# w2·h as seven products in the transform's stream, and gate/up over both token groups in one pass

## The chip, the cores and the metric

One core of a Trainium2 chip. The metric is device time in microseconds of one execution. Every matmul has 128-row operands, 512 moving columns and float32 data, taken as a high and a low float32r part: a product of two float32 tiles is three matmuls (high·high, high·low, low·high).

## The reference

```python
g = sigmoid((x * gate_w).sum(-1, keepdims=True))     # x: 2048 tokens x 512
a = Cr @ (x @ Dr.T) - Ci @ (x @ Di.T)                # C: 2048 x 2048, D: 512 x 512
b = (silu(x @ w1) * (x @ w3)) @ w2                   # w1, w3: 512 x 1376; w2: 1376 x 512
out = g * a + (1 - g) * b
```

## The kernel before, in words

Products are done in Winograd's form of Strassen's scheme: seven products of half-size blocks instead of eight, with sums of blocks as operands and sums of results behind them.

*Gate/up.* x is cut into two groups of 1024 tokens, w1 and w3 into NC = 11 chunks of 128 columns (the last is padded; the padding holds gate_w, so the scores for g come out of it). An item is one chunk and one group: seven products, 42 matmuls in PSUM tiles X, Y, Z, and ends in a tile h of 128 x 1024. `load_w`, `prep_wa` and `prep_wb` fetch and split an item's weight forms; `first1` and `first2` run its first two products three items (`LOOK`) ahead, `second` the other five. `split` writes a high part on ScalarE and a low part on VectorE. One operand set `XO` of x is kept, that of the current group.

*Down.* After the items of a group, `down(g)` runs w2·h in plain form: 11 chunks, each 8 accumulators (tile acc) x 3 matmuls, 264 matmuls a group. h (kept in SBUF) is split in `prep_dn`; the split w2 is kept in DRAM (`w2sp`) for the second group. acc is multiplied by 1 - g and stored to `nbsp`. Beside the first `down` the x operands of group 1 are made (x1 to x3), beside the second the x forms of the transform (`load_a`), the gates, and the first loads of its stream.

*The stream.* The transform runs as six blocks, `STEPS` in order: four F blocks (x with 512 columns of C, results to `zsp` in DRAM) and two Y blocks (hidden transform of what lies in zsp, plus nbsp, to out). A block has seven products P1, P5, P6, P3, P7, P2, P4 (Y blocks: P1, P2, P5, ...), a product NQ steps (4 in F, 2 in Y), a step 12 matmuls (2 banks x 2 slices of the contraction x 3). After step m `advance` issues loads for step m + 8 (`load_c`), sums for m + 4 (`sum_c`), and the split for m + 3 (`split_c`, into tile zo, four in turn). Loads go to tiles of the pool f4 (`wide`), 13 in turn. Operand names are B11, B12, B21, B22 (blocks), and T1 to T4 (sums). T1 is made by a load of B12 and an accumulating transfer of B11 on top, issued from POOL (F blocks: by VectorE); T2 and T4 are then summed in T1's tile by VectorE. P6 takes T2, P7 T3, P4 T4. `forms1` and `forms2` make the stationary forms (4 for P1, P5, P6, P3, 3 for P2, P4, P7).

*Order.* When the kernel is built, each engine's instructions are put in a queue by when their inputs and tiles should be ready, not strictly in program order. On the chip each queue runs in order. A new tile waits for the last use of the one whose place it takes. Loads are issued from SP's queue, accumulating transfers from POOL's.

The lines that the steps hang on:

```python
ORDER = [CHAIN] * NTB + [tuple(CHAIN[i] for i in (0, 5, 1, 2, 3, 4, 6))] * (NTB // 2)
NEED = [(("B11", 0, 0), ("B12", 1, 1), ("B22", 2, 1), ("B21", 5, 0))] * NTB + [
    (("B11", 0, 0), ("B21", 1, 0), ("T1", 2, 6), ("B22", 3, 1), ("T3", 5, 6))] * (NTB // 2)
LEAD = 3
AHEAD = 5
```

NEED lists for each load the product at which it is wanted and how many steps earlier it is put in.

Of the kernel before, what the change touches and what calls it, by code (L numbers as in the profile page):

```python
# [23 lines left out]
NC2 = (NC + 1) // 2  # L24
WARM = 11


@with_exitstack
def fnet_swiglu_gate_kernel(
# [18 lines left out]

    nc = tc.nc
# [13 lines left out]
    f4 = ctx.enter_context(tc.tile_pool(name="f4", bufs=13, side="right"))  # L63
    dn_cm, dn = pool("dn", 2, "right")
    xo_cm, xo = pool("xo", 1, "left")
    wo_cm, wo = pool("wo", 2, "left")
    tp_cm, tp = pool("tp", 2, "left")
# [3 lines left out]

    def wide(name):
        return f4.tile([P, 1024], F32, tag="f4", name=name)
# [13 lines left out]
    gsp = dram.tile([2, P, 1024], F32, tag="gsp", name="gsp")  # L87
    dsp = [dram.tile([KD, P, 2, n, 256], F32, tag=f"dsp{n}", name=f"dsp{n}") for n in (4, 3)]
    w2sp = dram.tile([NC, P, 2, 512], F32, tag="w2sp", name="w2sp")
    zsp = dram.tile([4 * NTB * P, 1024], F32, tag="zsp", name="zsp")  # L90

# [3 lines left out]
    def forms1(r, m, t1):  # L95

        r, m = (v.rearrange("p (a n) -> p a n", a=4) for v in (r, m))
        a21, a11, a12, a22 = (r[:, i] for i in range(4))  # L100
        nc.vector.tensor_sub(m[:, 0], a22, a21)
        for d, v, w in ((1, m[:, 0], a11), (2, a12, m[:, 1])):
            nc.vector.scalar_tensor_tensor(m[:, d], v, -1.0, w, op0=ALU.mult, op1=ALU.subtract)
        split(t1[:, 0, 0], t1[:, 1, 0], a11)
        split(flat(t1[:, 0, 1:4]), flat(t1[:, 1, 1:4]), flat(m[:, 0:3]))
# [8 lines left out]
    def prep_d(p):  # L114

        r, m = wide(f"dr{p}"), wide(f"dm{p}")
        t1 = dn.tile([P, 2, 4, 256], F32R, tag="ho", name=f"d1_{p}")
        t2 = dn.tile([P, 2, 4, 256], F32R, tag="ho", name=f"d2_{p}")[:, :, :3]
        nc.sync.dma_start(r, dd[p])
        forms1(r, m, t1)  # L120
        forms2(r, t2)
        nc.sync.dma_start(dsp[0][p], t1.bitcast(F32))
        nc.sync.dma_start(dsp[1][p], t2.bitcast(F32))


# [6 lines left out]
    def load_xo(g, k):  # L132

        if g not in XO:
            XO[g] = xo.tile([P, 2, 7, 2, 512], F32R, tag="xo", name=f"xo{g}")
        ST[g, k] = wide(f"xs{g}_{k}")
        nc.sync.dma_start(ST[g, k], xt[g, XRAW.index(k)])
# [4 lines left out]
    def sum_xo(g, k):  # L142
        ST[g, k] = wide(f"xs{g}_{k}")
        nc.vector.tensor_sub(ST[g, k], *(ST[g, v] for v in SUMS[k]))
# [6 lines left out]
    LOOK = 3  # L151

    def load_w(i, lo=0, hi=4, queue=nc.sync):
        if lo == 0:
            WS[i] = wo.tile([P, 4, 256], F32, tag="ws", name=f"ws{i}", bufs=LOOK + 1)
        queue.dma_start(WS[i][:, lo:hi].rearrange("p a n -> p (a n)"),
                          w13[i % NC, :, lo * 256 : hi * 256])

    def prep_wa(i, lo=0, hi=3):

        if lo == 0:
            WA[i] = wo.tile([P, 2, 3, 256], F32R, tag="wa", name=f"wa{i}", bufs=LOOK + 1)
        t = WA[i]
        split(t[:, 0, lo:hi].rearrange("p a n -> p (a n)"),
              t[:, 1, lo:hi].rearrange("p a n -> p (a n)"),
              WS[i][:, lo:hi].rearrange("p a n -> p (a n)"))

    def prep_wb(i, part=None):

        if part != 1:  # L170
            w = WS.pop(i)
            u = wo.tile([P, 4, 256], F32, tag="wu", name=f"wu{i}", bufs=1)
            nc.vector.tensor_add(u[:, 0], w[:, 3], w[:, 2])
            nc.vector.tensor_sub(u[:, 1], u[:, 0], w[:, 0])
            nc.vector.tensor_sub(u[:, 2], w[:, 0], w[:, 3])
            nc.vector.tensor_sub(u[:, 3], w[:, 1], u[:, 1])
            WB[i] = u
        if part != 0:
            u = WB[i]
            t = wo.tile([P, 2, 4, 256], F32R, tag="wb", name=f"wb{i}")  # L180
            split(t[:, 0].rearrange("p a n -> p (a n)"), t[:, 1].rearrange("p a n -> p (a n)"),
                  u.rearrange("p a n -> p (a n)"))
            WB[i] = t

    def prod(ps, i, wi, xi, start, chain=False):
        g = i // NC
        w, wi = (WA[i], wi) if wi < 3 else (WB[i], wi - 3)
        x = XO[g]
# [5 lines left out]
    G, H = {}, {}  # L194

    def first1(i):
        x = bank(i % 4, f"X{i}")
        prod(x, i, 0, 0, True)
        s1 = tp.tile([P, 512], F32, tag="s1", name=f"s1_{i}", bufs=LOOK + 2)
        nc.scalar.activation(s1, x, AF.Copy)  # L200
        G[i] = (x, s1)

    def first2(i):

        y = bank(4 + i % 2, f"Y{i}")
        prod(y, i, 1, 1, True)
        s1 = G[i][1]
        nc.vector.tensor_add(s1, s1, y)  # L208
        put_score(i, 0, s1)
# [4 lines left out]
    def put_score(i, j, gate):  # L214


        if i % NC < NC - 1:
            return
        if j == 0:
            SC[i] = tp.tile([P, 2, 512], F32, tag="sc", name=f"sc{i}", bufs=1)  # L220
        nc.scalar.activation(SC[i][F % P :, j], gate[F % P :], AF.Copy)
        if j == 1:
            nc.sync.dma_start(gs[2 * (i // NC) : 2 * (i // NC) + 2].rearrange("b o n -> o b n"),
                              SC[i][F % P : F % P + 1])

    def second(i, between):
        x, s1 = G.pop(i)
        z = bank(6 + i % 2, f"Z{i}")
        u2 = tp.tile([P, 512], F32, tag="u2", name=f"u2_{i}")
        u4 = tp.tile([P, 512], F32, tag="u4", name=f"u4_{i}")  # L230
        g1 = tp.tile([P, 512], F32, tag="g1", name=f"g1_{i}")
        h = wide(f"h{i}")
        H[i] = h
        prod(x, i, 4, 4, False, True)
        nc.scalar.activation(u2, x, AF.Copy)  # L235
        prod(z, i, 5, 5, True, True)
        nc.scalar.activation(u4, z, AF.Copy)
        between[0]()
        prod(x, i, 3, 3, False, True)
        nc.vector.tensor_add(u4, u4, x)  # L240
        prod(z, i, 2, 6, False, True)
        nc.vector.tensor_add(u2, u2, z)  # L242
        nc.vector.tensor_mul(h[:, :512], s1, u2)
        between[1]()
        prod(x, i, 6, 2, False, True)
        put_score(i, 1, x)
        nc.scalar.activation(g1, x, AF.Silu)  # L247
        nc.vector.tensor_mul(h[:, 512:], g1, u4)

    HO, W2R, W2O = {}, {}, {}  # L250

    def load_w2(i):

        if NC <= i < 2 * NC:
            W2O[i] = f4.tile([P, 2, 512], F32R, tag="f4", name=f"w2o{i}")
            nc.gpsimd.dma_start(W2O[i].bitcast(F32), w2sp[i - NC])

    def prep_dn(i):
        g, c = divmod(i, NC)
        if g == 0 and c % 2 == 0:  # L260
            n = min(2, NC - c)
            r = wide(f"w2r{i}")
            nc.sync.dma_start(r[:, : n * 512], w2[c // 2, :, : n * 512])
            W2R[i // NC, c // 2] = r
        if g == 0:
            o = dn.tile([P, 2, 512], F32R, tag="w2o", name=f"w2o{i}")
            split(o[:, 0], o[:, 1], W2R[g, c // 2][:, (c % 2) * 512 : (c % 2 + 1) * 512])
            nc.sync.dma_start(w2sp[c], o.bitcast(F32))
            W2O[i] = o
        t = dn.tile([P, 2, 1024], F32R, tag="ho", name=f"ho{i}")  # L270
        split(t[:, 0], t[:, 1], H.pop(i))
        HO[i] = t

    def down(g, extra):
        e = g * NC + NC - 1
        late = [6 + (e + 1) % 2, 6 + e % 2, e % 4]
# [458 lines left out]
```

## Time and profile before

| | before |
|---|---|
| median of three runs | 726.28 us (726.05 to 726.74) |
| profiled execution | 726.83 us |
| its span, first to last instruction | 725.0 us |
| TensorE busy, matmuls | 718.4 us, 3149 |
| VectorE, ScalarE, POOL busy | 542.6, 357.4, 27.1 us |
| moved by DMA | 136.60 MB |

In lines of groups the columns are: source line, engine, operation, output<-inputs with shapes, count | busy us in total, mean ns of one | idle time ahead of them and what ended it. Matmuls overlap, so the 389 ns of one is its latency, not its pace.

### The profile page before, as it was taken

What the parts mean: (1) busy time and instruction counts of PE and PEld (TensorE: products, weight loads), DVE (VectorE), ACT (ScalarE), POOL (GpSimd) and SP (SyncE); (2) the same over time, 40 slices, a digit from 0 to 9 for tenths busy, and PEclk for the clock granted to TensorE, in tenths of its full rate; (3) what the DMA queues carried; (4) which work ended last, traced back from release to release, by engine and by line L of the source; (5) the groups of instructions that cost most, each with busy time, mean ns of one, the idle gap of its engine ahead of it and who ended that gap; (6) DMA issues with size and microseconds to landing.
All of it is one profiled execution on the core that took longest, in us unless ns stands there. A gap on an engine that the chain in (4) does not pass through costs nothing.

```text
span 725.0 us, 8409 instructions
## 1 busy us (share of the span) xinstructions
PE 718.4 (99%) x3149; PEld 589.5 (81%) x3149; DVE 542.6 (75%) x676; ACT 357.4 (49%) x460; POOL 27.1 (4%) x39
## 2 busy tenths in 40 slices
PE   8999999999999999999999999999999999999997
PEld 5888878888888878888888888888888888888886
DVE  6987786584499974588978986687759785667875
ACT  6655454454466642553656345444444444445451
POOL 0000000000000000100010001000100001000000
PEclk9999999999999999999999999999999999999999
DMA  6112135733056601786897734874296719999932
GB/s 260 59 59 87 54 108 215 288 133 146 30 192 231 244 30 42 249 320 257 331 269 244 254 139 79 240 244 148 39 240 214 215 21 231 369 372 308 336 152 87
DMA packets 38780, 136.60 MB, mean 188 GB/s; under 512 B 4050, under 2 KB 4178, under 8 KB 37716
## 3 DMA queue, kind: packets, MB, share of 16 engines
q1 hardware_dynamic: 33412, 117.20, 45.3%
q0 software_dynamic: 5040, 18.35, 11.5%
q8 instruction: 24, 0.39, 0.2%
q10 hardware_dynamic: 288, 0.52, 0.2%
q14 instruction: 16, 0.13, 0.1%
HBM read 105.12 MB, written 30.94 MB: 188 GB/s over the span
## 4 chain that ended last, share of the span: by engine, by line
PE 90%; DMA 3%; DVE 3%; ACT 2%; issue 1%; SPq 0%; ACTq 0%; DVEq 0%
PE P L81 53%; PE acc L81 14%; PE X L81 13%; PE Z L81 6%; PE Y L81 3%; PE C L81 1%; DMA dsp<-d 1%; DMA xr<-xn 1%; DMA xs_B<-xt 1%; DMA gt<-gs 1%; ACT wb L76 0%; DVE ho L77 0%; DVE s L208 0%; DVE d L77 0%; DVE u L242 0%
## 5 line engine op out<-in xcount | busy, mean ns | idle before, releaser
L81 PE MATMUL P<-zo,a 128*128 128x512 f32 x1344 | 304.8, 389 | 0.0
L81 PEld LDWEIGHTS P<-zo,a 128*128 128x128 f32 x1344 | 252.2, 188 | 52.5 <-DVE zo L77 0.2
L76 ACT ACTIVATE zo<-B 128x1024 fp32r<-128x1024 f32 x124 | 131.3, 1060 | 148.2 <-PE P L81 142.0
L77 DVE TENSOR_TENSOR zo<-B,zo 128x1024 fp32r<-128x1024 f32 x124 | 150.7, 1222 | 65.9 <-ACT zo L76 65.3
L81 PE MATMUL acc<-ho,w2o 128*128 128x512 f32 x528 | 120.4, 389 | 0.1
L81 PEld LDWEIGHTS acc<-ho,w2o 128*128 128x128 f32 x528 | 99.0, 188 | 21.1 <-DVE ho L77 0.5
L81 PE MATMUL X<-xo,wb 128*128 128x512 f32 x378 | 94.4, 391 | 0.3
L81 PEld LDWEIGHTS X<-xo,wb 128*128 128x128 f32 x378 | 70.6, 188 | 16.6 <-ACT u L235 0.9
L81 PE MATMUL P<-zo,d 128*128 128x512 f32 x336 | 76.3, 389 | 0.0
L81 PEld LDWEIGHTS P<-zo,d 128*128 128x128 f32 x336 | 63.1, 188 | 13.1
L524 DVE TENSOR_TENSOR B<-B,B 128x1024 f32<-128x1024 f32 x48 | 58.3, 1222 | 5.9 <-DMA B<-cc 4.5
L76 ACT ACTIVATE wa<-ws 128x768 fp32r<-128x768 f32 (+2 forms) x23 | 18.8, 818 | 29.4 <-PE Z L81 27.9
L81 PE MATMUL X<-xo,wa 128*128 128x512 f32 x126 | 33.1, 391 | 0.0
L81 PE MATMUL Z<-xo,wb 128*128 128x512 f32 x126 | 32.3, 389 | 0.0
L81 PE MATMUL Y<-xo,wa 128*128 128x512 f32 x126 | 32.1, 389 | 0.0
L81 PE MATMUL Z<-xo,wa 128*128 128x512 f32 x126 | 32.0, 389 | 0.0
L77 DVE TENSOR_TENSOR wb<-wu,wb 128x1024 fp32r<-128x1024 f32 x21 | 25.7, 1225 | 7.1 <-ACT wb L76 6.9
L77 DVE TENSOR_TENSOR zo<-T,zo 128x1024 fp32r<-128x1024 f32 x16 | 19.6, 1223 | 12.4 <-ACT zo L76 12.4
L77 DVE TENSOR_TENSOR ho<-h,ho 128x1024 fp32r<-128x1024 f32 x22 | 26.9, 1221 | 1.7 <-ACT ho L76 1.7
L76 ACT ACTIVATE ho<-h 128x1024 fp32r<-128x1024 f32 x22 | 23.1, 1049 | 10.3 <-PE acc L81 8.8
L81 PEld LDWEIGHTS X<-xo,wa 128*128 128x128 f32 x126 | 23.5, 188 | 5.6 <-ACT g L247 0.4
L81 PEld LDWEIGHTS Z<-xo,wa 128*128 128x128 f32 x126 | 23.7, 188 | 5.0
(100 smaller groups left out, 591.5 us busy)
## 6 DMA issues: line engine op xcount, KB each, us to landing
B<-cc SPq DMA_DIRECT2D x64, 512.0 KB, 4.7
ws<-w SPq DMA_DIRECT2D x21, 512.0 KB, 3.7
B<-cc POOLq DMA_DIRECT2D x16, 512.0 KB, 5.5
B<-zsp SPq DMA_DIRECT2D x12, 512.0 KB, 11.0
w2sp<-w2o SPq DMA_DIRECT2D x11, 512.0 KB, 3.2
w2o<-w2sp POOLq DMA_DIRECT2D x11, 512.0 KB, 5.5
xs_B<-xt SPq DMA_DIRECT2D x8, 512.0 KB, 6.4
nbsp<-b SPq DMA_DIRECT2D x8, 512.0 KB, 3.3
```

The costliest lines, as they stand in the source:

```text
L76: nc.scalar.activation(hi, src, AF.Copy)
L77: nc.vector.tensor_sub(lo, src, hi.bitcast(F32))
L81: nc.tensor.matmul(ps, u, v, start=first and n == 0, stop=last and n == 2, skip_group_check=chain)
L524: nc.vector.tensor_add(t, t, RAW[blk, b, q])
```

## The change

w2·h becomes two blocks "H", one for each token group, between the F and the Y blocks. They use the seven-product scheme with 11 chunks as six in the first half of the contraction and five in the second. h is stored from gate/up to `hsp` in DRAM; w2's forms are made like those of the other matrices and kept in `w2sp`. `down`, `prep_dn` and their tiles go. Gate/up runs its 22 items in one pass: chunks 0 to 8 with group 0, chunks 9 and 10 with both groups, chunks 0 to 8 with group 1; both XO sets are in SBUF, and the wb forms of chunks 1 to 8 are stored in the first pass (`wbsp`) and loaded in the second. The x forms, and four of the six sets of w2 forms, are made beside the items (`A1_AT`, `W2_AT`); the other two and the four of the hidden transform beside F blocks 1 to 3 (`prep_late`). During gate/up the f4 pool has 4 tiles and zo 2, behind it 13 and 4. Stores of h and of kept forms are issued from POOL's queue.

```diff
+LOOK = 3
+K = 9
+XO_AT = 4
+W2_AT = (10, 11, 12, 20)
+A1_AT = (13, 14, 15, 16, 17, 18, 19)
...
+    F4 = [(f4_a, f"f4_{k}") for k in range(4)]
+    ZO = [(zo_a, f"zo_{k}") for k in range(2)]
+    def place(places):
+        places.append(places.pop(0))
+        return places[-1]
     def wide(name):
-        return f4.tile([P, 1024], F32, tag="f4", name=name)
+        p, tag = place(F4)
+        return p.tile([P, 1024], F32, tag=tag, name=name)
...
+    def keep_forms1(r, m, spill, p):
+        t = parts(f"k1_{spill[0].tensor.name}{p}")
+        forms1(r, m, t)
+        nc.gpsimd.dma_start(spill[0][p], t.bitcast(F32))
...
+    ITEMS = ([(c, 0) for c in range(K)] + [(c, g) for c in range(K, NC) for g in range(2)]
+             + [(c, 1) for c in range(K)])
...
+    def store_h(n, h):
+        c, g = ITEMS[n]
+        j = min(c % (NP2 - 1) if c < NC - 1 else NP2 - 1, NP2 - 1)
+        b = 2 * (NP2 - 1 <= c < NC - 1)
+        o = hsp[g, b : b + 2, j // 2, :, j % 2 * 512 : (j % 2 + 1) * 512]
+        nc.gpsimd.dma_start(o.rearrange("b p n -> p b n"), h.rearrange("p (b n) -> p b n", b=2))
...
-    def down(g, extra):
...
+    KIND = "F" * NTB + "HHYY"
+    ORDER = [CHAIN] * (NTB + 2) + [tuple(CHAIN[i] for i in (0, 5, 1, 2, 3, 4, 6))] * 2
+    NQ = [{"F": NG // 2, "H": NP2 // 2, "Y": KD // 2}[k] for k in KIND]
...
+    NEED = {
+        "F": (("B11", 0, 0), ("B12", 1, 1), ("B22", 2, 1), ("B21", 5, 0)),
+        "H": (("B11", 0, 0), ("T1", 1, 6), ("B22", 2, 1), ("T3", 4, 6), ("B21", 5, 0)),
+        "Y": (("B11", 0, 0), ("B21", 1, 0), ("T1", 2, 6), ("B22", 3, 1), ("T3", 5, 6)),
+    }
+    PLACE = {"F": {"T1": "B12", "T2": "B12", "T4": "B12", "T3": "B22"},
+             "H": {"T2": "T1", "T4": "T1"}, "Y": {"T2": "T1", "T4": "T1"}}
...
+    def cols(blk, q, form):
+        return 512 if KIND[blk] == "H" and q == NQ[blk] - 1 and form in ("B21", "B22", "T4") else 1024
...
+    close(*gate_pools)
...
+    F4[:0] = [(f4_b, f"f4_{k}") for k in range(4, 13)]
+    ZO[:0] = [(zo_b, f"zo_{k}") for k in range(2, 4)]
+    make_a(NG - 1, a1b)
+    advance(-1)
...
+    for p in range(NG):
+        at(0, 2 * p, load_a2, p)
+    at(0, 0, gates, 0)
+    at(1, 1, gates, 1)
...
+    for p in range(NP2):
+        at(NTB, p - 3 * NQ[0], load_forms, "H", 0, p, w2sp, p)
+        at(NTB, p + 1, load_forms, "H", 1, p, w2sp, p)
```

More of the change, by code (lines that the diff above doesn't have):

```diff
@@ L244, in second @@
         between[1]()
-        prod(x, i, 6, 2, False, True)
-        put_score(i, 1, x)
+        prod(x, n, 6, 2, False, True)
+        put_score(n, 1, x)
         nc.scalar.activation(g1, x, AF.Silu)
[L248 to L272, printed above, removed]
@@ new lines, in fnet_swiglu_gate_kernel, with prep_w2 @@
+    extra[XO_AT] = [lambda: split_xo(1, "B11")]
+    extra[XO_AT + 1] = [lambda: split_xo(1, "B21")]
+    extra[XO_AT + 2] = [xo_sum("T1", "B11")]
+    extra[XO_AT + 3] = [xo_sum("T2", "B11")]
+    extra[XO_AT + 4] = [xo_sum("T3", "B12")]
+    extra[XO_AT + 5] = [xo_sum("T4", "B21"), lambda: split_xo(1, "B22")]
+    def prep_w2(p):
+        r, m = wide(f"w2r{p}"), wide(f"w2m{p}")
+        nc.sync.dma_start(r, w2[p])
+        keep_forms1(r, m, w2sp, p)
+        keep_forms2(r, w2sp, p)
+    A1, A2, XR = [], [], {}
@@ L622, in step @@
             for n, zn in steps:
-                for i in range(2):
+                for i in range(ni):
                     w = ws[2 * n + i]
```

520 lines of the change are left out of this document (261 added, 259 removed).

## The prediction

> **What bounds the kernel now.** The page's head comes first: span, busy times, and the chain that ended last by engine.
>
> ```profile
> span 725.0 us, 8409 instructions
> ...
> PE 718.4 (99%) x3149; PEld 589.5 (81%) x3149; DVE 542.6 (75%) x676; ACT 357.4 (49%) x460; POOL 27.1 (4%) x39
> ...
> PE 90%; DMA 3%; DVE 3%; ACT 2%; issue 1%; SPq 0%; ACTq 0%; DVEq 0%
> ```
>
> TensorE is busy for 99% of the span and nine tenths of the chain is its own. The chain in order of time gives its pace, and what lies before and behind it.
>
> ```profile
> 9.97 5.81 PE C L81 x24
> ...
> 114.37 59.88 PE acc L81 x264
> ...
> 340.23 380.86 PE P L81 x1680
> ...
> 721.12 0.69 DVE zc L584
> ```
>
> The first real matmul runs at 9.97 us, the last ends at 721.1. The transform's 1680 matmuls take 380.86 us without a gap, 0.2267 us each; the 264 of a w2 pass cost the same (59.88/264 = 0.2268). So matmuls are paid by number. All 3138 behind the 11 warming ones make 711.4 us, and 9.97 + 711.4 = 721.4: there is no idle time of TensorE worth naming. Its list of waits agrees:
>
> ```profile
> PE wps L344 <- DVE warm L341: 1.2, 1, 1.2
> PE C L81 <- ACT xo L76: 0.6, 1, 0.6
> PE C L81 <- DVE xo L77: 0.5, 2, 0.3
> ```
>
> All three lie in the start. So a change gains 0.2267 us for each matmul removed, and pays for each moment at which TensorE has to wait, for which there is no slack to hide in.
>
> **Term 1: matmuls removed.**
>
> ```profile
> L81 PE MATMUL acc<-ho,w2o 128*128 128x512 f32 x528 | 120.4, 389 | 0.1
> ```
>
> These 528 go. A block H of the stream has seven products of six 128-row steps of the contraction; the three that read the second half alone (forms B21, B22, T4) have five. That is 4 x 6 + 3 x 5 = 39 steps, times 6 matmuls: 234 a block, 468 in two. Gate/up, F and Y blocks keep their counts, as the built kernel's own list does (3089 matmuls instead of 3149). The gain is 60 x 0.2267 = 13.6 us. It is certain, and the most that the change can bring.
>
> **Term 2: operands of the H blocks.** h now goes to DRAM and comes back into the 13 tiles that `wide` deals out in turn, and TensorE's moving operands lie in four `zo` tiles, also in turn. Reading off who gets whose tile: the list of loads of block 4 is T1 (3), B11 (3), B22 and T3 (6), B21 (3), that is 15 loads for 13 tiles. So B21_1 goes into the tile of T1_0, B21_2 into that of T1_1, and the next block's T1_0 into that of T1_2. But T1 is kept until the last product, P4: T1 becomes T2 and then T4 = T2 + B21 in place. P4's step 0 must therefore be split before B21_1 can even be loaded, and B21_1 is wanted for P2's step 1. The built queues show it: VectorE has P4's step 0 ahead of P2's step 1, and TensorE alternates the two products there. F blocks (16 loads) do not have this, their tiles come free a whole product before they are wanted; Y blocks have P2 second. Durations for the chain:
>
> ```profile
> L76 ACT ACTIVATE zo<-B 128x1024 fp32r<-128x1024 f32 x124 | 131.3, 1060 | 148.2 <-PE P L81 142.0 <-issue 3.7 <-DMA B<-cc 2.2
> L77 DVE TENSOR_TENSOR zo<-B,zo 128x1024 fp32r<-128x1024 f32 x124 | 150.7, 1222 | 65.9 <-ACT zo L76 65.3
> L524 DVE TENSOR_TENSOR B<-B,B 128x1024 f32<-128x1024 f32 x48 | 58.3, 1222 | 5.9 <-DMA B<-cc 4.5 <-DVE B L524 0.6
> L639 ACT ACTIVATE zu<-P 128x512 f32<-128x512 f32 x24 | 14.4, 599 | 15.0 <-PE P L81 15.0
> L656 DVE TENSOR_TENSOR zp<-zp,zu 128x1024 f32<-128x1024 f32 x6 | 7.3, 1221 | 5.0 <-ACT zu L639 5.0
> L77 DVE TENSOR_TENSOR w2o<-w2r,w2o 128x512 fp32r<-128x512 f32 x11 | 7.6, 689 | 10.0 <-ACT w2o L76 10.0
> L643 DVE TENSOR_TENSOR zs<-zs,P 128x512 f32<-128x512 f32 x12 | 7.7, 679 | 0.0
> L577 DVE TENSOR_TENSOR zs<-zs,gate 128x512 f32<-128x512 f32 x8 | 5.1, 682 | 0.0
> ```
>
> and for the transfers (KB each, median us from issue to landing):
>
> ```profile
> B<-cc SPq DMA_DIRECT2D x64, 512.0 KB, 4.7
> ws<-w SPq DMA_DIRECT2D x21, 512.0 KB, 3.7
> B<-cc POOLq DMA_DIRECT2D x16, 512.0 KB, 5.5
> B<-zsp SPq DMA_DIRECT2D x12, 512.0 KB, 11.0
> w2sp<-w2o SPq DMA_DIRECT2D x11, 512.0 KB, 3.2
> ...
> T<-zsp SPq DMA_DIRECT2D x8, 512.0 KB, 11.6
> T<-zsp POOLq DMA_DIRECT2D x8, 512.0 KB, 9.4
> ...
> gate<-gsp SPq DMA_DIRECT2D x4, 256.0 KB, 5.6
> ```
>
> Let t = 0 be the end of P7's last matmul, which frees the zo tile of P4's step 0. ScalarE first reads P7's two banks (2 x 0.6 = 1.2), VectorE adds them (1.22, to 2.4), then finishes the split: 3.6. B21_1 is issued and lands at 3.6 + L1. VectorE then does a sum, the split of P2's step 1 and that of P4's step 1, 3 x 1.22: T1_1 is free at 7.3 + L1, and B21_2 (256 KB) lands at 7.3 + L1 + L2. A half sum and a half split follow, 2 x 0.69: 8.7 + L1 + L2. Ten matmuls (2.3 us) are then still to come: P4 ends at 11.0 + L1 + L2. From t = 0 TensorE had 60 matmuls to do, 13.6 us. The stall is L1 + L2 - 2.6.
>
> Which L? The bounds are 3.2 (the fastest row of this size, a store) and 11.0 (loads from DRAM scratch). The latter is taken in stretches in which all 16 DMA engines are full:
>
> ```profile
> 340.00:417.00 77.00, 77.00 (x342) 63.63 (x341) 65.22 (x80) 40.52 (x53) 3.53 (x4) 1.00 0.86 281
> 417.00:493.00 76.00, 76.00 (x337) 62.94 (x336) 56.24 (x54) 33.91 (x37) 3.46 (x4) 1.00 0.60 178
> 646.00:684.00 38.00, 38.00 (x170) 31.45 (x169) 29.59 (x28) 19.13 (x23) 5.21 (x6) 1.00 1.03 330
> ```
>
> (Behind the length: busy us of TensorE's matmuls and weight loads, VectorE, ScalarE, POOL; the last two columns are the DMA share and GB/s.) The first of these is F block 0, the second F block 1, the third a Y block. In the H blocks the weight forms of the next stage are issued some 10 us ahead of B21_1, and nothing big comes behind it, so I take the unloaded 4.7 for both: the stall is 6.8 us a block. [...]
>
> Behind P2 in block 4, VectorE takes the two sums and two gate products of P2's banks (4 x 0.68 = 2.7) before the first operand of block 5: another 2.2 us. Then T1_0 of block 5, issued behind P4's last split at 9.4 + L1 + L2: 4.7 + 5.5 for the added transfer + 1.06 + 1.22 make 12.5 us, so it is ready at 21.9. TensorE is through with P1 at 11.0 + 2.2 + 36 x 0.2267 = 21.4 (both plus L1 + L2): 0.5 left. In block 5 the order of the Y block puts P2's operands first, which covers the sums; T1_0 of block 6 stands behind another load on POOL, 1 us left. Sum: 6.8 + 2.2 + 0.5 and 6.8 + 1.0, **17.3 us** (11 with L at 3.7; over 50 with 11.0 and 11.6 + 9.4 everywhere).
>
> **Term 3: the seam from gate/up to the stream.** Before, the second w2 pass hid the x forms, B11, B12 and the sums of T1. Now the stream follows the last gate matmul directly. SP's queue holds a load of x into the room of the second x operand set, which waits for that matmul; behind it stand B11_3 and the four B12. TensorE has 46 matmuls of P1, 10.4 us. The fourth B12 or third sum needs about five loads in a row, and VectorE then has a split, two small ones, three sums and the split for P5 in its order: about 12.5 to 13 us. I take 3 us with what follows (VectorE is at 65.2 of 77 us in F block 0 above, and gets some 8 us more), bounds 0 to 8.
>
> **Edits at nothing.** h's stores replace the ho splits; the forms of w2 and of the hidden transform move to gate/up and into blocks 1 to 3, where VectorE has 20 us free (56.24 of 76) and takes some 8. In gate/up VectorE gets the second x set, 11 operations of 1.22, and one set of w2 forms:
>
> ```profile
> 20.00:114.00 94.00, 93.84 (x412) 76.56 (x411) 79.89 (x126) 51.93 (x77) 0.00 (x0) 1.00 0.24 80
> ```
>
> That adds at most 13.4 + 4 us to a stretch in which VectorE is busy for 79.89 of 94 us, 14 free, ahead of TensorE by three items: I take 0 (up to 4 if it falls behind). The second pass's eight evacuations of acc lay beside the first products of F, and cost nothing before either. One more seam: B11_0 and B11_1 of block 4 get the tiles of the last two T forms of block 3, and have 13.6 us (five steps) less a split each way (2 x 2.4) to land, 8.8 us, between the rows 4.7 and 11.0. I take 1 us, bounds 0 to 4.
>
> **The sum.** 725.0 - 13.6 + 17.3 + 3 + 1 = 732.7 us of span. The profiled execution took 726.83 us, 1.83 beside its span, and lies 0.55 above the median of 726.28. So 734.5 for a profiled run and **734.0 us** for the median, 1.1% slower.
>
> **Rivals.**
> A, faster: the refill of the H blocks is short. The mechanism is the same chain, and the price its L: at 3.2 for both loads the stall is 3.8 a block, T1_0 is covered, and with both seams covered 734.0 - 2 x 3.0 - 1.5 - 4 = 722.5 us. It decides from L1 + L2 of about 7.5 down, with the seams at 0. For it: TensorE's waiting stops the other consumers too, so that DMA has nothing else to do. Against it: ws at 3.7 is the fastest load of 512 KB. [...] Should a tile come free earlier than I read, the stall is gone and the time is 734.0 - 17.3 = 716.7, less again without seams; I see no way for that in the queues.
> B, crowded DMA: two H blocks, the forms of w2 (10.5 MB) and of the Y stage (7 MB) come in some 110 us together with stores. If B21 lands as B<-zsp does and T1_0 as the T<-zsp rows do, a block pays 14.0 (11.0 + 5.6 - 2.6) and 11 more at T1_0, 36 us above the forecast in all, 770; halfway is 752. For it the Y stretch with a share of 1.03; against it that my count of bytes just ahead of B21_1 (about 3 MB in 11 us) is below what the chip moves in the quoted windows.
> C, POOL's queue becomes the bound of gate/up: eight items put out h (512 KB) and the kept forms (1 MB) there, with two h tiles. If these went one after another at 5.5 us each, 11.0 stands against an item's 42 x 0.2267 = 9.5: 8 x 1.5 = 12 us, 746. Against it this row, two transfers issued within 1.79 us, so a transfer does not hold the queue until it lands:
>
> ```profile
> 372.37 1.79 POOL L535 DMA_DIRECT2D B<-cc  x2 [2.62 <-ACT zu L639]
> ```
>
> That the change doesn't do what it says is excluded by the count of matmuls.
>
> **How the numbers follow.** Forecast 0.68, A 0.13, something between A and the forecast that ends at no change 0.04, B 0.10, C 0.05. A difference of 0.2% (1.45 us) is what a measurement can tell from none: faster 0.13, same 0.04, slower 0.83. The range goes from A's 722.5 to 750, short of B's half-way value.
>
> **What would show it.** Right: TensorE's list of waits names P (H blocks) behind VectorE and DMA twice, about 6 to 9 us each where P2 and P4 alternate, with the loads of B21 from the h scratch just before; a shorter wait at the first P5 operand of F block 0; the gate/up and F stretches as long as their matmuls; 3089 matmuls. Wrong: TensorE without a gap at P2 and P4 (term 2 falls, the time is then 717); large waits in gate/up (C, or VectorE); waits that end at T transfers rather than B21 (B); landing times of the h loads near 3 us (A).

## The result, and the profile after

The changed kernel takes 816.61 us (median of four, 815.57 to 817.99) against 726.22 us for the kernel before on the same chip: a ratio of 1.1244 (95% interval 1.1225 to 1.1264). The forecast was 734.0, range 722.5 to 750. The direction was right, the size was not: 83 us are missing from it. The profiled execution took 817.12 us, of which the span is 815.3.

The head of the page, with the granted clock and the DMA share in 40 slices of the span:

```profile
span 815.3 us, 8580 instructions
...
PE 748.3 (92%) x3089; PEld 592.5 (73%) x3089; DVE 564.2 (69%) x705; ACT 368.0 (45%) x485; POOL 67.7 (8%) x96
...
PEclk9999999989899999999999999989999789888999
DMA  6766832787829888638953996499999864984924
```

Three things differ from before. TensorE is idle for 8% of the span instead of 1%. Its matmuls, 60 fewer, are *busy* for longer, 748.3 us instead of 718.4. And the granted clock, which never left 9 before, falls below it in eight of the 40 slices. The list of TensorE's waits, led by three rows that did not exist before:

```profile
PE P L108 <- ACT zo L103: 39.8, 12, 8.4
PE P L108 <- DVE zo L104: 12.6, 14, 3.3
PE X L108 <- ACT h L297: 4.3, 1, 4.3
```

What a wait does to the clock is seen in windows around the longest one of gate/up, 7.25 us up to 222.90 (columns behind the window: its length, TensorE's busy time and matmuls, granted clock, DMA share, GB/s):

```profile
215.00:217.50 2.50, 0.65 (x3) 1.00 1.00 424
217.50:220.00 2.50, 0.00 (x0) 0.54 0.81 341
220.00:222.50 2.50, 0.00 (x0) 0.50 0.08 33
222.50:225.00 2.50, 2.10 (x5) 0.50 0.55 210
225.00:227.50 2.50, 2.50 (x7) 0.50 0.00 0
227.50:230.00 2.50, 2.50 (x12) 0.91 0.00 0
```

The clock falls to 0.50 while TensorE waits, and stays there for about five microseconds of work: from 225.0 to 227.5, six matmuls start where eleven would at the full clock (the x7 counts those that touch the window). TensorE counts as busy there, so no list of waits contains this loss.

With the start times of the 3089 matmuls and the clock records of the trace the whole time can be parted. Each interval from one start to the next is 0.2267 us, plus what the half clock adds, plus a slower pace at full clock, or it is a wait. (From start to start a wait counts some 0.17 us more than in the list, which begins at the end of a matmul.)

| us beyond 0.2267 a matmul: waits / half clock / pace | gate/up | F | H | Y | sum |
|---|---|---|---|---|---|
| forecast | 0 / 0 / 0 | 3 / 0 / 0 | 17.3 / 0 / 0 | 1 / 0 / 0 | 21.3 |
| after | 18.1 / 5.2 / 3.3 | 23.2 / 5.5 / 3.9 | 27.7 / 10.7 / 1.3 | 4.0 / 3.1 / 1.2 | 107.1 |
| ring | 17.0 / 3.5 / 3.3 | 23.6 / 4.6 / 3.9 | 0 / 0 / 1.4 | 0.2 / 0 / 1.3 | 58.8 |
| forms_sp | 11.5 / 1.6 / 3.4 | 16.9 / 4.8 / 4.2 | 30.9 / 10.3 / 1.3 | 5.9 / 2.8 / 1.2 | 94.6 |
| align2 | 16.8 / 6.0 / 0.2 | 25.0 / 4.8 / 0.3 | 30.0 / 7.9 / 0.3 | 8.5 / 2.4 / 0.2 | 102.4 |
| best5 | 8.6 / 1.6 / 0.4 | 18.7 / 4.4 / 0.6 | 4.3 / 1.8 / 0 | 1.4 / 0 / 0 | 41.6 |
| no_late | 16.7 / 4.0 / 0.5 | 8.6 / 1.6 / 0.1 | 0.2 / 0 / 0 | 2.4 / 0 / 0 | 34.0 |
| no_forms | 6.6 / 1.7 / 0.3 | 7.4 / 1.8 / 0.1 | 2.1 / 0 / 0 | 5.1 / 1.6 / 0 | 26.9 |

(The kernel before has 3.4 us of waits and 0.5 of pace in its start and first stage by the same count, and nothing else. Sums may differ by 0.1 from rounding. The other rows are experiments, below.)

So of the 107.1 us, 73.0 are waits, 24.5 half clock and 9.6 pace. The forecast had 21.3 of waits, and nothing of the other two.

Where the waits come from is read in the chain in order of time. In H block 4 it is the path of the prediction, with a longer transfer:

```profile
626.55 1.23 DVE zo L104
...
627.79 9.92 DMA B<-hsp
...
637.74 1.07 ACT zo L103
...
638.85 1.22 PE P L108 x2
```

Behind it come the two transfers of the next block's T1_0 in a row. They are read from the queues of SP and POOL:

```profile
648.21 0.32 SPq L529 DMA_DIRECT2D T<-hsp  x1
...
651.98 0.32 SPq L529 DMA_DIRECT2D T<-zsp  x1
...
656.24 0.88 POOL L533 DMA_DIRECT2D T<-hsp  x1 [7.45 <-DMA T<-zsp]
```

The load lands after 7.4 us, at 655.6; the added transfer is issued then and lands after 7.6, at 663.8. POOL's line, and the chain with it, names T<-zsp as the releaser, a load for a Y block. That is inferred, and wrong here: this load lands after 6.2 us, at 658.2, when the added transfer has long begun.

In gate/up and F it is mostly the stores of the kept forms. The split of the stream's first operand, whose first matmuls stand in TensorE's queue among the last gate items, has to wait for a zo tile that such a store holds (it lands after 13.5 us, at 221.7); in block 3 the same with a store of 14.47 us:

```profile
208.19 10.85 DMA w2sp<-k_w2sp
...
221.79 1.06 ACT zo L103
...
222.90 1.22 PE P L108 x2
...
530.73 14.47 DMA dsp<-k_dsp
...
545.82 1.05 ACT zo L103
```

### The profile page after: what moved, and what is told of

Read it like the earlier page. It is cut to its first block, busy times and chain, and to the rows that moved or that the text cites. A ratio compares the mean times of both kernels' runs of the same rounds, so it can differ in the third digit from the quotient of the medians.

```text
span 815.3 us, 8580 instructions
## 1 busy us (share of the span) xinstructions
PE 748.3 (92%) x3089; PEld 592.5 (73%) x3089; DVE 564.2 (69%) x705; ACT 368.0 (45%) x485; POOL 67.7 (8%) x96
## 3 DMA queue, kind: packets, MB, share of 16 engines
q0 software_dynamic: 13024, 58.73, 24.5%
## 4 chain that ended last, share of the span: by engine, by line
issue 31%; PE 27%; DMA 23%; DVE 12%; ACT 3%; POOL 3%; SPq 0%; POOLq 0%; ACTq 0%; DVEq 0%
PE P L108 23%; DVE zo L104 5%; DMA dsp<-k_dsp 5%; DMA B<-hsp 3%; DMA w2sp<-k_w2sp 3%; PE X L108 2%; DMA T<-zsp 2%; DMA xr<-xn 2%; ACT zo L103 2%; DMA B<-zsp 2%; DMA xs_B<-xt 2%; DMA B<-cc 1%; PE Z L108 1%; POOL hsp L276 1%; DMA T<-hsp 1%
## 5 line engine op out<-in xcount | busy, mean ns | idle before, releaser
L108 PEld LDWEIGHTS P<-zo,a 128*128 128x128 f32 x1344 | 254.9, 191 | 90.1 <-ACT zo L103 18.7
L103 ACT ACTIVATE zo<-B 128x1024 fp32r<-128x1024 f32 (+1 forms) x142 | 146.3, 1044 | 184.5 <-PE P L108 83.6
L104 DVE TENSOR_TENSOR zo<-B,zo 128x1024 fp32r<-128x1024 f32 (+1 forms) x142 | 169.3, 1205 | 75.5 <-ACT zo L103 75.5
L108 PE MATMUL P<-zo,H 128*128 128x512 f32 x468 | 121.8, 422 | 24.1 <-ACT zo L103 21.4
L108 PEld LDWEIGHTS P<-zo,H 128*128 128x128 f32 x468 | 93.6, 203 | 51.9 <-ACT zo L103 25.6
L108 PE MATMUL P<-zo,Y 128*128 128x512 f32 x336 | 81.4, 404 | 3.3 <-ACT zo L103 2.7
L108 PEld LDWEIGHTS P<-zo,Y 128*128 128x128 f32 x336 | 65.0, 194 | 19.7 <-ACT zo L103 3.1
L104 DVE TENSOR_TENSOR zo<-T,zo 128x1024 fp32r<-128x1024 f32 (+1 forms) x40 | 47.7, 1195 | 36.2 <-ACT zo L103 36.0
L103 ACT ACTIVATE zo<-T 128x1024 fp32r<-128x1024 f32 (+1 forms) x40 | 41.2, 1035 | 51.8 <-PE P L108 28.1
L509 DVE TENSOR_TENSOR T<-T,B 128x1024 f32<-128x1024 f32 (+1 forms) x20 | 22.2, 1116 | 22.6 <-DMA B<-hsp 22.3
L108 PEld LDWEIGHTS X<-xo,wa 128*128 128x128 f32 x126 | 24.3, 194 | 11.5 <-ACT h L297 4.7
L685 ACT ACTIVATE zu<-P 128x512 f32<-128x512 f32 x32 | 18.7, 594 | 27.0 <-PE P L108 27.0
L290 DVE TENSOR_TENSOR u<-u,X 128x512 f32<-128x512 f32 x21 | 14.4, 683 | 21.8 <-PE X L108 21.6
L108 PEld LDWEIGHTS Z<-xo,wa 128*128 128x128 f32 x126 | 24.5, 195 | 5.7
## 6 DMA issues: line engine op xcount, KB each, us to landing
T<-hsp SPq DMA_DIRECT2D x12, 512.0 KB, 11.2
```

The costliest lines, as they stand in the source:

```text
L103: nc.scalar.activation(hi, src, AF.Copy)
L104: nc.vector.tensor_sub(lo, src, hi.bitcast(F32))
L108: nc.tensor.matmul(ps, u, v, start=first and n == 0, stop=last and n == 2, skip_group_check=chain)
L509: nc.vector.tensor_add(t, t, RAW[blk, b, q][:, :n])
L685: nc.scalar.activation(U[name][:, r], ps[r], AF.Copy)
```

## The experiments

**The wait alone (before_waits).** In the kernel before, the low part of a split is computed several times over at six places:

```diff
         split(t[:, 0], t[:, 1], src)
+        for _ in range(SLOW.get((blk, m - START[blk]), 0)):
+            nc.vector.tensor_sub(t[:, 1], src, t[:, 0].bitcast(F32))
```

> The kernel before, in which VectorE repeats the low part of one operand's split 7 to 13 times (1.22 us each, the same values again) at six places of the stream's blocks 1 to 3: 8 and 10 times in block 1, 7 and 11 in block 2, 9 and 13 in block 3, so that TensorE has six waits of graded length and nothing else is changed. With some 7 us of lead, waits of about 1.5 to 9 us are to be expected, 25 to 32 us together. Theory (a wait of TensorE costs more than itself, because the granted clock falls to 0.5 for some 3.4 us or a multiple behind waits of about 4 us and more): the granted clock falls behind the three or four longest and not behind the shortest, and the time grows by the waits and another 5 to 14 us: 757 to 772. Rival (the clock falls from the crowded memory or the work of the changed kernel, not from the waits): the granted clock stays at 1.0 throughout and the time grows by the waits alone, 752 to 758.

755.27 us (ratio 1.0402, 1.0364 to 1.0439). The planned order put the repeats between other splits, so that the waits came in two lengths, not six: three of 3.69 us and the rest of 0.4 to 1.64. Behind one of the long ones, and behind one of 1.04 us at 430.47:

```profile
468.90:472.50 3.60, 0.00 (x0) 0.88 0.63 226
472.50:475.00 2.50, 2.45 (x6) 0.50 0.68 252
475.00:477.50 2.50, 2.50 (x8) 0.50 0.70 236
477.50:480.00 2.50, 2.50 (x11) 0.81 0.01 3
...
427.50:430.50 3.00, 1.96 (x10) 1.00 0.00 0
430.50:433.00 2.50, 2.50 (x11) 1.00 0.00 0
```

The three long waits cost 3.41, 1.71 and 3.41 us of clock (half of the time at 0.50, of which a part passes while TensorE still waits), the short ones none. Of the 29.2 us by which the stream grew, 21.4 are waits and 7.4 half clock. The time by itself lies in the rival's range, 752 to 758, because the waits came to less than the 25 to 32 us that were planned; what decides is the clock, which the rival had at 1.0 throughout. The theory holds in a kernel with none of the changed kernel's traffic: the wait does it. In the clock records of the changed kernel the stretches at 0.50 last 3.41, 6.83 or 10.24 us, so that each loss is a multiple of 1.71, less what passes while TensorE waits. How long a wait has to be is not settled: the changed kernel lost clock behind each of its nine waits of 1.67 to 8.42 us (1.71 behind that of 1.67, up to 721.3). Elsewhere, waits of 2.00 (no_forms, up to 276.3) and 2.27 us (best3, up to 603.1) lost 1.7 us, while those of 2.11 (no_forms, up to 240.3) and 2.32 (best4, up to 595.9) lost none. Two short waits in a row did it as well: 1.43 and 1.56 us in the changed kernel, up to 302.0, with the clock at 0.50 from 303.1 to 306.5.

**The H blocks: another order (h_order).**

```diff
-    ORDER = [CHAIN] * (NTB + 2) + [tuple(CHAIN[i] for i in (0, 5, 1, 2, 3, 4, 6))] * 2
+    ORDER = [CHAIN] * NTB + [tuple(CHAIN[i] for i in (0, 5, 1, 2, 3, 4, 6))] * 4
-        "H": (("B11", 0, 0), ("T1", 1, 6), ("B22", 2, 1), ("T3", 4, 6), ("B21", 5, 0)),
+        "H": (("B11", 0, 0), ("B21", 1, 0), ("T1", 2, 6), ("B22", 3, 1), ("T3", 5, 6)),
```

> The changed kernel with the two H blocks in the Y blocks' order (P1, P2, P5, P6, P3, P7, P4), so that B21 is loaded for the second product and no tile has to come free of P4 first; the gate tile is loaded at P2 instead of P6. Nothing else differs. Theory (the ring of 13 tiles is what stalls the H blocks): the waits of TensorE in and right behind the H blocks, 8.4 + 1.3 + 4.9 + 0.5 + 5.1 + 1.7 + 2.7 + 0.5 = 25 us, fall under 6 us, and the half-clock stretches behind them (17 us of lost clock) with them: about 816.6 - 19 - 14 = 780 us (772 to 790). Rival (the transfers themselves are too slow: B<-hsp lands at a median of 9.7 us and T<-hsp at 11.2): the waits move to the T1 and T3 operands and their sum stays within 6 us of 25; the time stays above 808.

811.01 us (1.1170, 1.1137 to 1.1202): closer to the rival. But the chain shows what the waits, now one of 12.9 and one of 12.4 us, hang on:

```profile
627.61 1.15 DVE zo L104
...
628.77 6.64 DMA T<-hsp
...
636.06 6.92 DMA T<-hsp
...
643.00 1.06 ACT zo L103
...
644.11 1.22 PE P L108 x2
```

Both waits stand before matmul 192 of their block's 234, where the last step of P7 begins. The operand of that step, T3_2, is loaded at the moment when the split of P4's step 0 is done: with 15 loads dealt out to 13 tiles in turn, it gets the tile of T1_0, which P4 holds. Three shorter waits, 6.9 us together, end with loads of w2's forms, which P2, now second, wants earlier. So the edit did not do what it was meant to do. The circle was not broken by it, it moved.

**The H blocks: another choice of tile (ring).** Order as in the changed kernel; `pick` takes the tile whose last use comes first.

```diff
-            r = RAW[blk, k, q] = wide(f"{k}_{blk}_{q}")
+            r = RAW[blk, k, q] = pick(f"{k}_{blk}_{q}", LASTUSE[blk, k, q], blk > 3)
```

> The changed kernel with another choice of tile for the loads of the H and Y blocks alone: each load takes, of the 13 tiles, the one whose last use comes first, instead of the next in turn. The order of products is that of the changed kernel. Theory (the prediction's: B21_1, B21_2 and the next block's T1_0 were given tiles that P4 itself still holds): the waits in and right behind the H blocks (8.4 + 1.3 + 4.9 + 0.5 + 5.1 + 1.7 + 2.7 + 0.5 = 25 us) fall to under 7 us and 17 us of lost clock behind them to under 4: about 816.6 - 18 - 13 = 785 us (775 to 793). Rival (the loads themselves are too slow where the forms of w2 are loaded too, as in the run with the Y order, whose waits moved to T<-hsp and H<-w2sp): at least 15 us of waits stay in the H blocks, and the time above 800.

770.67 us (1.0609, 1.0581 to 1.0637), 46 us less, for an edit that moves no work. It beat the theory's 775 to 793, which had left some waits. First the H blocks of ring with the landing time of the loads of h (median, last column), then the same of the changed kernel:

```profile
577.50:685.00 107.50, 107.50 (x469) 1.00 1.00 328
...
B<-hsp SPq DMA_DIRECT2D x14, 512.0 KB, 12.5
```

```profile
580.30:726.10 145.80, 121.66 (x470) 0.90 0.84 278
...
B<-hsp SPq DMA_DIRECT2D x14, 512.0 KB, 9.7
```

Not one wait is left in the H blocks, at a DMA share of 1.00 and 328 GB/s: more traffic than in the changed kernel, where the share was 0.84, and loads that land later still, after 12.5 us instead of 9.7. So crowded DMA makes no wait here by itself. It sets how long a transfer in the circle takes; without the circle that costs nothing.

**The matmul's pace (align, align2, before_pad).** In the changed kernel, stretches without a wait and at full clock went at 0.232 us a matmul instead of 0.227. Sorted by operand, nearly all matmuls of xo0 were slow (0.2333 us from start to start between 25 and 100 us) and most of those of xo1 fast (0.2267 between 175 and 215), with weights in the same tiles. Their addresses differ: tiles on the left of SBUF, xo0 among them, begin at a multiple of 128 bytes, those on the right, xo1 and the weights of gate/up among them, 64 bytes past one.

```diff
-    act0 = const.tile([P, 1], F32, tag="act0", name="act0")
+    act0 = const.tile([P, 216], F32, tag="act0", name="act0")[:, :1]      # align2; align: [P, 32]
```

> The changed kernel with one edit of memory only: the constant tile at the top of SBUF is 128 bytes long instead of 4 (it takes 64 of them as allocated before), so that every tile on the right side of SBUF begins 64 bytes lower. In the changed kernel as it stands the first x operands, two of the zo tiles and seven forms begin at a multiple of 128 bytes, and the weights of gate/up, the second x operands, the other two zo tiles and the other forms 64 bytes beside one; the kernel before paired only tiles of the same kind. Theory (a matmul whose moving operand and weights lie differently to 128 bytes takes 0.233 us from start to start instead of 0.227: the changed kernel has 508 matmuls in the undisturbed 118 us from 32 to 150 us, 0.232 each, against 835 in 189.84 us before, 0.227): all matmuls at full clock go at 0.227, the stretch from 32 to 150 us holds some 518 of them, and the time falls by about 9 us to 807.6 (804 to 811); waits stay within a few us. Rival (the slower pace comes from the crowded memory or from small waits that the profile does not list): pace and time stay, 815 to 818 us.

> The changed kernel with one edit of memory only: the constant tile at the top of SBUF takes 864 bytes a partition, so that all tiles on the right side begin at the same remainder to 2048 as those on the left, as in the kernel before. (In the run align the allocator rounded the first edit to 96 bytes, and the two sides stayed unlike; the pairs of zo tiles on the right with forms on the left, of which half went at 0.233 us in the changed kernel, nearly all did there.) Theory (a matmul whose moving operand and weights begin at unlike remainders goes at 0.233 us from start to start instead of 0.227): the stretch from 32 to 150 us comes to 0.227 to 0.228 a matmul (518 of them in 118 us instead of 508), and the time falls by about 9 us to 807.5 (803 to 811). Rival (pace set by how far apart the tiles lie, or by traffic): no change, 815 to 818.

> The kernel before with 64 bytes a partition of padding behind the x operands, so that the weights of gate/up begin 64 bytes beside a multiple of 128 while the x operands stay at one; a short write to the padding by POOL is the only instruction added. Theory (unlike remainders cost 6.6 ns a matmul): the 924 matmuls of gate/up go at 0.233 us, the rest at 0.227: 726.3 + 6.1 = 732.4 us (730 to 734). Rival: 726.3, no change.

A stretch of gate/up, first in the changed kernel, then in align and align2:

```profile
38.00:150.00 112.00, 112.00 (x485) 1.00 0.55 204
```

```profile
38.00:150.00 112.00, 112.00 (x485) 1.00 0.55 201
```

```profile
38.00:150.00 112.00, 112.00 (x495) 1.00 0.58 210
```

And in the kernel before, without and with the 64 bytes:

```profile
30.00:110.00 80.00, 79.84 (x350) 1.00 0.25 83
```

```profile
30.00:110.00 80.00, 79.96 (x343) 1.00 0.21 70
```

align was a miss of the edit: the right side moved by 96 bytes, the sides stayed unlike, and the time too (817.15 us; 1.1239, 1.1209 to 1.1268). With equal remainders align2 has 495 matmuls where 485 went, 0.2263 us each, with more traffic beside them. The edit of the kernel before does the reverse: 343 for 350, and 731.06 us (1.0057, 1.0035 to 1.0078), 4.7 more, where 6.1 were expected; by the starts of its matmuls the pace takes 6.1 us where it took 0.5, and waits in the start are 1.5 shorter. For the pace the theory holds both ways, and traffic is ruled out. The time of align2, 812.45 us (1.1170, 1.1133 to 1.1206), falls by 4.2 rather than 9 and misses the theory's 803 to 811: its waits grow by 7.3 in the table. That fits a TensorE that goes faster and meets the same late operands, but was not tested by itself.

**The stores of the kept forms (forms_sp, no_item20).** The first stores them from SP's queue instead of POOL's; the second moves the w2 set of item 20 to F block 0.

```diff
-        nc.gpsimd.dma_start(spill[0][p], t.bitcast(F32))
+        nc.sync.dma_start(spill[0][p], t.bitcast(F32))
...
-W2_AT = (10, 11, 12, 20)
+W2_AT = (10, 11, 12)
```

> The changed kernel with the stores of the kept forms of w2 and of the hidden transform issued from SP's queue instead of POOL's; h's stores stay on POOL. Theory Q (POOL's queue is the bound, as in rival C of the prediction: h's stores stand behind the stores of the forms, and these land late, 8.8 and 6.9 us on POOL where the w2 pass of the kernel before had 3.2 on SP): the waits at 174.7 (4.26 us), 222.9 (7.25) and 546.9 (5.46) shrink to under 2 us each, with the half clock behind them: about 816.6 - 13 - 9 = 795 us (788 to 803). Theory D (the DMA engines are full there: share 1.0 at 420 to 440 GB/s from 155 to 175 us): the wait near 175 stays at 3 us or more, and loads that now stand behind the stores on SP add waits; 810 to 830 us.

> The changed kernel with the w2 set of item 20 moved out of gate/up into steps 17 to 23 of F block 0 (three sets stay at items 10 to 12). Theory (the first two operands of the stream are split early into the only two zo tiles, and wait for the stores of the kept forms of item 20 that hold them; their matmuls stand in TensorE's queue among the last gate items): the wait of 7.25 us at 222.9 goes, with about 4 us of half clock behind it; the wait at 174.7 (4.26 us) stays; F block 0 gets up to 5 us of new waits; about 806 us (803 to 813). Rival (it is the load of the first operands that comes late in a crowded memory): the wait at 222.9 stays over 4 us and the time within 4 us of 816.6.

forms_sp: 804.90 us (1.1085, 1.1053 to 1.1118), between the two theories. The wait at 222.9 shrank to 1.0 and that at 546.9 to 2.5 us; the one at 174.7 gave way to one of 4.0 at 170.1. The stores land sooner from SP; the large ones of w2's sets in the changed kernel and in forms_sp (median, last column):

```profile
w2sp<-k_w2sp POOLq DMA_DIRECT2D x6, 1024.0 KB, 8.8
...
w2sp<-k_w2sp SPq DMA_DIRECT2D x6, 1024.0 KB, 6.4
```

no_item20: 806.24 us (1.1104, 1.1035 to 1.1172), as the theory had it; the wait at 222.9 is gone, that near 174 is still 4.7. For this one the chain of the changed kernel shows a store of a kept form (8.87 us), then a load of x (9.68), then ScalarE, which has the split of that load ahead of h in its queue; forms_sp shows 6.23 and 5.72 us and VectorE in the same part. POOL's queue is not the reason: POOL stands idle for 9.31 us ahead of h's store at 175.79. The DMA engines are full there:

```profile
155.00:160.00 5.00, 3.94 (x18) 1.00 1.01 396
160.00:165.00 5.00, 4.53 (x19) 1.00 0.97 304
165.00:170.00 5.00, 3.90 (x17) 1.00 1.02 421
170.00:175.00 5.00, 0.74 (x4) 0.83 1.03 436
```

Three sets in a row are 3 x 1.75 MB stored and 1.5 MB loaded within 30 us, on top of h, which goes out, and the wb forms, which come back, in any case.

**Leaving the forms out (no_forms, no_late).** Both have ring's choice of tile and align2's addresses.

> The changed kernel with the tile choice of the run ring and the like remainders of the run align2, and with no kept forms at all: the six sets of w2 and the four of the hidden transform are neither loaded, made nor stored, and the H and Y blocks load the wb forms of gate/up in their place (so w2 and the hidden transform are left out of the result; matmuls, and loads of forms in number and size, are the same). Theory (the kept forms are what makes gate/up and F wait): gate/up loses its waits at 160 to 175 and at 221 (17 us of waits in that stage fall under 5, with 3.5 us of half clock), F falls from 23.6 us of waits to under 10, with most of its 4.6 us of half clock: 770.7 - 9 - 16 - 18 = 728 us (718 to 736). Rival (the waits come from the rest: h and wb through DRAM, the seam without a w2 pass): at least 25 us of waits stay in the two stages together, above 745 us.

> As no_forms, but the four w2 sets of gate/up (items 10, 11, 12 and 20) are kept and stored as in the changed kernel; only the six sets made beside F blocks 1 to 3 are left out (the loads of the H and Y blocks take the four sets that are there). Theory: F as in no_forms, gate/up with its waits (4 us at 174, 7 us at 221): 12 to 18 us above no_forms. Rival (the forms made in F are the dear ones, those of gate/up cheap): under 6 us above no_forms.

734.64 us (1.0088, 1.0060 to 1.0117) and 746.08 us (1.0262, 1.0226 to 1.0298). F takes 336.8 us in ring and 315.0 in no_late; 3.8 of the 21.8 between them are pace, so the late sets cost F 18.0. The four sets of gate/up cost that stage 12.5 (232.0 against 219.5). no_forms lies in its theory's range, no_late 11.4 above it, just under the 12 to 18 that were expected: the forms make most of what gate/up and F waited. With them gone TensorE is idle for the start, as before, and for the rest of the change alone:

```profile
PE P L108 <- DVE zo L104: 7.2, 7, 2.1
PE P L108 <- DMA Y<-wbsp: 4.6, 2, 3.3
PE X L108 <- ACT h L297: 2.3, 3, 2.0
```

That is the most telling number of the study. With its forms for nothing, its tiles well chosen and its matmuls at full pace, the changed scheme still takes 0.9% longer than the kernel before. The stream's start without a second w2 pass, h and wb through DRAM and the loads of forms eat what 60 matmuls bring; how they divide was not tested.

**Putting the forms elsewhere (best_q, best_kt, best3, best4, best5).** These keep all the work and add edits: ring's choice, for F blocks 1 to 3 too, fewer w2 sets in gate/up, the rest beside F, x's second forms and the gates of block 0 some steps later, stores from SP in the stream; from best_kt on a tile of their own for kept forms, from best3 on align2's addresses.

```diff
-        blk, n = 1 + i // 2, 1 + i % 2 * 8
+        blk, n = ((1, 3), (1, 11), (1, 19), (2, 3), (2, 11), (2, 19), (3, 3), (3, 11))[i]      # best5
...
+    kt_cm, kt = pool("kt", 1, "right")                     # best_kt on: kept forms of the stream
```

> Several edits together on the changed kernel: tiles alike to 128 bytes (as in align), every load of the stream in the tile whose last use comes first, the w2 sets of gate/up at items 10, 12 and 16 (each with its A1 moved on) and the fourth in F block 0, kept forms stored from SP's queue in the stream and from POOL's in gate/up, the second forms of x and the gates of block 0 two and three steps later. Theory (four separate causes that add): align 9, the ring 31, the gate/up waits at 174.7 and 222.9 with their clock 18, the F waits 10: about 750 us (740 to 765), still above the kernel before. Rival (the time is bound by the bytes, 196 MB against 137 before, and waits come back elsewhere): above 775.

> As best_q, and the kept forms of the stream get a tile of their own (8 KB a partition), for which the F blocks have 11 tiles for loads instead of 13 until four steps ahead of the H blocks. Theory (a kept form takes a turn of the four zo tiles and holds it until its store has landed, which delays the operand behind it): the waits inside F blocks 1 to 3 that end with ACT zo or DVE zo (some 13 us with their clock in the changed kernel) go almost entirely: 5 to 8 us below best_q. Rival (eleven tiles are too few for the loads of F, so that waits on B<-cc take their place): 0 to 15 us above best_q.

> best_kt with like remainders (align2), only two w2 sets in gate/up (items 10 and 12, A1 as in the changed kernel), and the other four with the four of the hidden transform beside F blocks 1 to 3 (three, three, two), none in block 0. Theory (causes add): against best_kt's 762.4 the pace gives 12, the wait of 5.0 us at 189.9 with 3 of clock and that of 4.7 at 314 with 3 of clock go: about 736 us (730 to 748). Rival (VectorE and DMA of blocks 1 and 2 become too full with three sets each): new waits there, 748 to 765.

> best3 with a third w2 set in gate/up (items 10, 11, 12, as in the changed kernel but without the one of item 20), so that F blocks 1 to 3 have three, two and two. Theory: three sets in a row fill the DMA engines again from 155 to 175 us (share 1.0 in the changed kernel), the wait of 4 to 5 us near 174 comes back with 2 to 3 of clock, and block 2 is relieved: 3 to 8 us above best3. Rival: POOL's stores alone were the cause and the wait stays away; at or below best3.

> best3 with the eight sets of kept forms of F blocks 1 to 3 put two steps later each (steps 3, 11 and 19 of a block instead of 1, 9 and 17), so that the first is not made while block 0 still ends: there ScalarE, in its fixed order, waited 4.1 us for the raw w2 of the first set in best4, and the wait of 3.5 us at 309.5 followed. Theory: that wait and its half clock go, 4 to 7 us below best4's 756. Rival (the set is put ahead by the planned order wherever it is written): 750 to 762, the wait stays.

best_q 768.65 us (1.0581, 1.0560 to 1.0602), best_kt 762.40 (1.0495, 1.0474 to 1.0516), best4 755.98 (1.0402, 1.0368 to 1.0436), best5 752.46 (1.0350, 1.0329 to 1.0371); best3 took 749.8 and 762.7 in its two runs, too far apart to be placed, and both above its theory's 730 to 748. The tile of their own gave the 6 us that were expected, but only in part where they were expected: the waits behind ACT zo fell from 3.3 to 1.1, those behind DVE zo stayed (8.9 and 9.4), and more came from one wait for ScalarE in F block 0, outside the theory (ACT zu, 8.0 and 4.7). best_q lay between theory and rival: the waits that its edits took away came back in part elsewhere. In best4 the wait of the third set in a row came back too, 4.1 us at 171.0, as its theory had it. Two more are instructive. In best_kt's gate/up ScalarE, whose queue is fixed when the kernel is built, had the split of the stream's first operand ahead of an eviction; its load took 9.13 us instead of the time planned for:

```profile
179.04 9.13 DMA B<-cc
...
188.27 0.04 ACT zo L103
...
189.23 0.59 ACT u L294
```

And in best4 it waited for raw w2 while block 0 was still to be finished:

```profile
ACT k_w2sp L103 <- DMA u3p<-w: 4.1, 1, 4.1
```

best5 moved that set; the wait of 3.5 us was still 3.2 at 306.8, as its rival had it, and the gain came from gate/up, which has a set fewer than in best4, and elsewhere in F. No version came below the kernel before.

## Why the prediction was wrong

Of the 82 us by which the span missed the forecast, the table puts 35 on waits in gate/up and F that were put at nothing (*Edits at nothing*), 24.5 on the half clock, which no term had, 13 on waits in the H and Y blocks that were longer than forecast (*Term 2*), and 9 on pace. The steps one by one:

- *Bound and term 1* (TensorE never waits, each removed matmul gains 0.2267 us): right for the 60, but the sentence that matmuls are paid by number was not a property of the matmul. It held because the kernel before pairs operands and weights of like address. The change puts them on both sides of SBUF: 9.6 us where 0.5 stood before, and no term had it.
- *Term 2* (the circle through the tiles): the mechanism was right, and ring shows that it was all there was to the H blocks. In the list, the wait before B21 in block 4 was 8.4 us (6.8 forecast) and the next 1.3 (2.2), in block 5 5.1 + 1.7 (6.8). L for B21_1 was 9.92 and 6.57 instead of 4.7, so the choice of the "unloaded" row was wrong: something big did come behind it, a set of Y forms (768 KB) that SP issued at 630.01, and the DMA share of the H blocks was 0.84. B21_2, of half the size, took 4.7 and 3.7, as forecast or less, which made up for L1 in block 5. The mis-sized part is T1_0 of the next block: 4.9 + 0.5 where 0.5 was forecast, as its two transfers took 7.4 + 7.6 instead of 4.7 + 5.5. Of the whole, 25.1 listed against 17.3.
- *The step that was missing*: every wait was priced at its own length. The half clock behind it adds 24.5 us in all, 13.8 of them in the H and Y blocks, where the waits themselves are 31.7. In the profile of before nothing shows it, as its longest wait is 1.2 us. But the clock column was there, and the price of a wait that the kernel has not had yet was an unknown to be bounded.
- *Edits at nothing*, the step that cost most: 18.1 us of waits in gate/up and 23.2 in F where 0 and 3 were forecast (some 3 of the 18.1 lie in the start, and did before). VectorE's busy time was counted, and it was not the bound. What was not counted is who holds a tile how long: two zo tiles in gate/up, four in F, each held by a kept form until its store lands, 5 to 14 us. no_late and no_forms put 18.0 and 12.5 us on these forms, half clock included.
- *Term 3*: the wait at the first P5 operand was 3.27 us at 258.4, forecast 3. Right, and by the path that was named: the load of x at 243.69, then the loads of B, a sum and a split. *Seam from F to H*: 1.4 + 0.8, forecast 1.
- *Rival A* falls: the loads of h landed after 9.7 (B) and 11.2 us (T) in the median. *Rival B* had these landing times nearly right (11.0, and 11.6 + 9.4), but not the waits, 14.0 and 11 us a block; ring shows that slow transfers cost time only through the circle. *Rival C* named the right stage, for 5% at 12 us, but not the reason: POOL issued the two stores of item 20's set within 0.9 us (207.36 and 208.19), so its queue was not held; they held their tiles until they landed, after 9.6 and 13.5 us. In forms_sp, which gained 11.7 us, the same two landed after 8.0 us at most. No rival's time came near 816; the highest was B's 770.

What stays open: how the remaining waits of F in best5 (18.7 us) divide between planned order and late loads, what decides whether a wait of some 2 us brings the half clock, and which remainder of addresses counts. Shown unlike are 64 bytes of 128 (before_pad, after) and 96 (align); shown alike are equal remainders to 2048 (before, align2).

## What to carry to other kernels

Where TensorE is full, price a new wait at its length plus 1.7 to 3.4 us for the half clock behind it, which is what each of the changed kernel's nine waits of 1.67 us and more lost. That is an estimate: some of up to 2.32 us in other runs lost none. By it ten waits of 3 us are dearer than one of 30, a length that no run had. When buffers go round in turn, write down for each load which earlier use it waits for, in the new order too: a choice of tile by last use was worth 46 us here without moving any work. And a form that is kept by a store holds its tile until the store lands, 5 to 14 us here: count tiles and landing times, not only the engine's busy time.

## What the runs showed of the hardware

- Matmuls of 512 columns whose moving operand and weights begin at unlike remainders (64 bytes of 128) went at 0.233 us from start to start, those at like remainders at 0.227 (gate/up in before_pad and in before): 343 against 350 in 80 us. Where part of them were unlike, 485 started in 112 us against 495 with all alike (the changed kernel and align2).
- In the changed kernel the granted clock fell to 0.50 behind all nine waits of 1.67 us and more, and behind two pairs of shorter ones (1.43 + 1.56 up to 302.0, 1.42 + 0.76 up to 585.9). In best3, best4, best5, no_forms and no_late it did so behind every wait of 2.64 us and more, and behind some of about 2 us but not all (2.27 in best3, but not 2.32 in best4).
- The stretches at 0.50 in the changed kernel lasted 3.41, 6.83 or 10.24 us, each 3.41 costing 1.71 us of work where none of it passed while TensorE still waited.
- The DMA engines moved 328 GB/s for 107.5 us at a share of 1.00 without TensorE waiting once (ring).
- Stores of 1 MB landed after 8.8 us in the median when POOL issued them (the changed kernel), and after 6.4 when SP did (forms_sp).
